# First units of a gated attention and routed experts kernel: one transfer for the second set of decay operands, narrower gate arithmetic, loads and gate rows in another order

## The chip, the cores and the metric

The kernel runs as one program on 1 core of one Trainium2 chip. The metric is the device time in microseconds (us); the median of the runs is compared. Engines are called PE (matmul; PEld is its weight load), DVE, ACT and POOL; SP only issues DMA transfers. POOL issues transfers too.

## The reference, cut to what matters

Two stages follow one another. The first is a gated linear attention over 4 batches, 8 heads, 768 steps and head size 40, with a stabiliser that runs along time:

```
for t in range(S):
    m_new = np.maximum(f_gate[:, :, t] + m, i_gate[:, :, t])
    f_stab = np.exp(f_gate[:, :, t] + m - m_new)
    i_stab = np.exp(i_gate[:, :, t] - m_new)
    C = f_stab * C + i_stab * np.einsum('bhd,bhe->bhde', vt, kt)
    n = f_stab * n + i_stab * kt
    h_tilde = np.einsum('bhde,bhe->bhd', C, qt)
    denom = np.maximum(np.abs(nq), 1.0)
    y[:, :, t] = o * h_tilde / denom
```

The second takes the 3072 rows of y (320 wide) to the best two of 8 experts each: noisy logits, a softmax over the two, `relu(x @ w1[e]) @ w2[e]` with a hidden width of 1024, weighted and added up.

## The kernel before, in words

**Units.** Time is cut into chunks of 64 steps. A unit is one chunk of two batches, so there are 24 units: 0 to 11 for the first pair of batches, 12 to 23 for the second. The loop over `i` runs unit `i` and prepares the next ones. What a unit needs: queries and keys `qk` (two transfers, 256 and 64 KB, line 170), values and keys `vk` (two of 162 KB, one from SP and one from POOL, line 175), the output gate `og` (160 KB, line 177). Each has four buffers; in the loop unit `i + 3` is loaded in iteration `i`. Buffers of `qk` are blanked once (`blank`, line 191), those of `vk` get zeros and unit matrices once (lines 263 to 268).

**Work of a unit, in PE's order.** `c_part` (line 381) makes the next state, `o_part` (390) the outputs, `e_part` (330) the decay exponents of unit `i + 2` in two halves, each followed by an Exp on ACT (333) that makes the weights `w`; `l_part` and `t_part` (433, 413) belong to the experts' logits; `s_part` (353, 350) makes the scores of unit `i + 2`. DVE makes `kd` (361, keys times the last decay of `w`), the three steps of the denominator (395 to 401) and the weighted scores `p` (367, or 371 for a pair's first unit). `o_part(i)` waits for `p` of its unit, `c_part(i)` for `kd`. ACT also makes the sigmoid of `og` in three steps (`sig_part`, 339), POOL the finished rows (402), which are sent off on line 405. Each engine takes its instructions in the order in which the program writes them.

**Gates.** `gate_math` (lines 212 to 234) turns f and i gates into decay sums: two scans and six other steps on DVE, eight in all, for a stretch of time, into `HL`. `gate_move` (line 236) takes 128 steps of `HL`, that is two units, to the operands `LE` and `RE` with three small transfers (16, 8 and 8 KB). `RE` and `LE` have two sets, used in turn, two units each. The constant part of a set, which never changes, is written once: `operands` (248, 250) on ACT, `heads` (257 on ACT, 259 on DVE). Before, the set of units 2 and 3 is filled by ACT and DVE as the first is. Gate stretches are 128 wide for the first two and 256 wide for the last two; the latter's steps are a generator, `gates2`, of which the loop takes some at places that `GATES` sets.

**Names in the rows.** `e(u)` below means the decay matmuls of unit `u`; the row `e<-re,le` of line 330 appears twice for each unit.

**Order and waits.** Nothing is reordered: the order of the program is that of each engine. Each queue issues in order, and an issue that waits holds back all behind it. Warm-up matmuls on zeros (line 712, `WARM`, `WARM2`, `WARM3`) fill PE at the start. After the units the experts follow, the first of which is begun in the last units' iterations.

Of the kernel before, what the change touches and what calls it, by code (L numbers as in the profile page):

```python
# [7 lines left out]
F32 = mybir.dt.float32  # L8
# [5 lines left out]
AF = mybir.ActivationFunctionType  # L14
OP = mybir.AluOpType
AX = mybir.AxisListType

B, H, S, D = 4, 8, 768, 40
NE, F, DM = 8, 1024, 320
L = 64  # L20
# [19 lines left out]
NR = NE - EF  # L40

STEP, SHARE = 0.19, 1.65
WARM, WARM2, WARM3 = 16, 5, 2
GATES = {0: 5, 2: 4, 3: 4}
LEAD = 2
TURN = 6
OR1 = (0, 6, 1, 2, 3, 4, 5)
# [5 lines left out]
GC = 2  # L53
# [12 lines left out]
def build(ctx, tc, qk, vk, og, fi, noise, wgn, w1, w2, cst, ce, out):  # L66
# [98 lines left out]
    def load_unit(u, what="kvg"):  # L165
        pr, c = divmod(u, NCH)
        if "k" in what:
            r = 0
            for a, step, n in DIMS:
                SP.dma_start(QK[u % 4][a:128:step], qk[pr, c, r:r + n])  # L170
                r += n
        if "v" in what:
            flat = VKS[u % 4].rearrange("p x c -> p (x c)")
            for p in range(2):
                (P if p else SP).dma_start(flat[64 * p:64 * p + 64, VW * p:VW * p + 648], vk[pr, c, p])
        if "g" in what:
            SP.dma_start(SG[u % 4], og[pr, c])
# [12 lines left out]
    def blank(i, q):  # L190
        q.memset(QK[i], 0.0)
# [8 lines left out]
    SP.dma_start(fit[:, :, 128:256], fi[:, :, 128:256])  # L200
    load_unit(0, "k")
    SP.dma_start(cs[:, 0:C_TRI], cst[:, 0:C_TRI])
    load_unit(0, "vg")
    P.dma_start(fit[:, :, 256:512], fi[:, :, 256:512])
    blank(2, P)

    def run(steps):
        for _ in steps:
# [29 lines left out]
    def gate_move(kk, q=(SP, SP)):  # L238
        pr, k = divmod(kk, GB)
        j = kk % 2  # L240
        src = HL[32 * pr:32 * pr + 32, :, k * GC * L:(k + 1) * GC * L].bitcast(F32)
        q[0].dma_start(LE[j][64:96, :, 64:128].bitcast(F32), src[:, 0].rearrange("r (c t) -> r c t", c=GC))
        for x in range(2):
            q[x].dma_start(RE[j][96 + x:97 + x].bitcast(F32), src[16 * x:16 * x + 16, 1])

    def operands(j, p, eng=None):
        if p is None:
            A.activation(LE[j][0:KE], cet[0:KE, None, E_L:E_L + 192].to_broadcast([KE, GC, 192]), AF.Copy)
        else:
            A.activation(RE[j][0:64, p].rearrange("r h (c t) -> r h c t", c=GC),  # L250
                         cet[0:64, None, None, 0:L].to_broadcast([64, H, GC, L]), AF.Copy)

    def heads(j, p, eng):
        o, i = RE[j][64:96, p], cet[64:96, E_H:E_H + H, None].to_broadcast([32, H, GC * L])
        x = cet[64:96, E_P + p:E_P + p + 1]
        if eng is A:
            A.activation(o, i, AF.Copy, scale=x)
        else:
            V.tensor_scalar(o, i, x, None, op0=OP.mult)


    def key_zeros(i):
        P.memset(VK[i][1][32:64, 0:328], 0.0)
# [2 lines left out]
    def keys(i):  # L266
        P.tensor_copy(VK[i][0][64:104, 328:648].rearrange("p (h d) -> p h d", h=H), ident[64:104, None, 64:104].to_broadcast([40, H, D]))
        P.tensor_copy(VK[i][1][0:64, 328:648].rearrange("p (h d) -> p h d", h=H), ident[0:64, None, 0:D].to_broadcast([64, H, D]))
# [5 lines left out]
    gate_move(0, (SP, P))  # L274
    operands(0, 0, A)
    operands(0, 1, A)
    heads(0, 0, A)
    heads(0, 1, A)
    load_unit(1)
    keys(0)  # L280
    keys(1)
    operands(1, None, A)
    operands(1, 0, A)
    run(gate_math(GC * L, 256))
    heads(1, 0, V)
    heads(1, 1, V)
    gate_move(1, (SP, P))
    load_unit(2, "k")
    blank(3, P)
    for i in range(2, 4):  # L290
        key_zeros(i)
        keys(i)
    load_unit(2, "vg")
    load_unit(3, "k")

    def constants():
        P.memset(W1L[0:64, 2].bitcast(F32), 0.0)
# [26 lines left out]
    def e_part(u, ps_=(0, 1), first=False):  # L324
        pr, c = divmod(u, NCH)
        j = (GB * pr + c // GC) % 2
        c = c % GC
        for p in ps_:
            ps = XTB if first and p else psum.tile([128, 512], F32, name="e")
            T.matmul(ps, LE[j][0:KE, c, 64 - 64 * p:192 - 64 * p], RE[j][0:KE, p, :, c * L:c * L + L], start=True, stop=True)  # L330
            if p == 0:
                W[u] = wk.tile([128, 2, H, L], F32, name="w", bufs=LEAD)
            A.activation(W[u][:, p].rearrange("p h t -> p (h t)"), ps, AF.Exp)  # L333

    def sig_part(u, ps_=(0, 1, 2)):

        g = SG[u % 4]
        for p in ps_:
            A.activation(g, g, (AF.Exp, AF.Ln, AF.Exp)[p], bias=float(p == 1), scale=(-1.0, 1.0, -1.0)[p])
# [4 lines left out]
    def s_part(u):  # L344
        q = QK[u % 4]
        for h in range(H):
            if whole(u) and h == 1:
                for p in range(2):
                    r = qrow[p]
                    T.matmul(SQ[u][:, p][r], cs[r, C_DIM:C_DIM + 64], q[r, 0], start=True, stop=True)  # L350
            for p in range(2):
                r = qrow[p]
                T.matmul(SQ[u][:, p][half[p], h, :], q[r, 1, h, :], q[r, 0, h, :], start=True, stop=True)  # L353
# [4 lines left out]
    def k_part(u):  # L358
        if u % NCH < NCH - 1:
            KD[u] = wk.tile([128, 2, H, D], F32, name="kd")  # L360
            V.tensor_mul(KD[u], VKS[u % 4][:, :, 328:648].rearrange("p x (h d) -> p x h d", h=H),
                         W[u][:, :, :, L - 1:L].to_broadcast([128, 2, H, D]))
# [346 lines left out]
    def warm(n):  # L709
        wp = psum.tile([128, 512], F32, name="o")  # L710
        for _ in range(n):
            T.matmul(wp, wz[:, 0:128], wz, start=True, stop=True)
# [3 lines left out]
    s_room(1)  # L716
    s_part(0)
    warm(WARM2)
    e_part(0, first=True)
    operands(1, 1, A)  # L720
    warm(WARM3)
    s_part(1)
    e_part(1, first=True)
    k_part(0)
    p_part(0)
    load_unit(3, "vg")
    SP.dma_start(fit[:, :, 512:], fi[:, :, 512:])
    SP.dma_start(wgt, wgn)
    gates2 = (s for t0 in (256, 512) for s in gate_math(t0, t0 + 256))

    def route(i):
        if 2 <= i <= NU + 1 and sum(GROUPS[GOF[i - 2]]) == i - 1:
# [93 lines left out]
    i = 0  # L826
    while i < NU - LEAD:
        unit[0] = i
        spent[0] = 0.0
        if 1 <= i and i + 3 < NU:  # L830
            load_unit(i + 3, "kv")
        if i:
            keep_rows(i - 1)
        if 1 <= i and i + 3 < NU:
            load_unit(i + 3, "g")
        if i % 2 == 0 and i and i // 2 + 2 < 2 * GB:
            gate_move(i // 2 + 2, (P, P) if i < XV else (SP, SP))

        if i in W1LD:
            piece_w1(W1LD.index(i))  # L840
        if i == W2AT:
            early_w2(0, 4)
        if i == 4:
            SP.dma_start(cs[:, C_TRI:], cst[:, C_TRI:])
        if i == 5:
            SP.dma_start(nzt, noise)
        while sent:
            SP.dma_start(*sent.pop())
        if not begun and done[0] >= E0U[0]:
            decode(0, E0S[1] // 128, 128 * E0U[0] > FIT)  # L850
            begun = 1
        if begun and late < len(tiles(0, 0)):
            gather(0, 0, tiles(0, 0)[late:late + 2])
            late += 2
            begun = 2
        if i == 6:
            constants()
            A.activation(spot, cs[:, C_N:C_N + 128], AF.Copy)
            A.activation(tri, cs[:, C_TRI:C_TRI + 128], AF.Copy)
            A.activation(ones, cs[:, C_ONE:C_ONE + 128], AF.Copy)  # L860
        asked = len(acts)
        k_part(i + 1)
        if i == 1:
            for _ in range(8 - GATES[0]):
                next(gates2)
            gate_move(2, (SP, P))
        fill(0.2, False)
        s_room(i + 2)
        c_part(i)
        if i:  # L870
            sig_part(i + 1, (0,))
        o_room(i)
        o_part(i)
        e_part(i + LEAD, (0,))
        act(asked)
        if i == 0:
            sig_part(0)
        f_part(i, lambda: fill(0.15, False))
        p_part(i + 1)
        t = l_part(i)  # L880
        w = r_part(t)
        b = None if w else b_part(t)
        if i:
            t_part(i - 1)
            tc_part(i - 1)
        lc_part(i, t, w)
        bc_part(t, b)
        if i < 2:
            s_part(i + 2)
            sig_part(i + 1, (1, 2) if i else (0, 1, 2))  # L890
            e_part(i + LEAD, (1,))
        else:
            e_part(i + LEAD, (1,))
            s_part(i + 2)
            act()
            sig_part(i + 1, (1, 2))
        route(i)
        fill((SHARE if i < NU - 3 else 0.6) - spent[0])
        if i in W1AT:
            next(pre1)  # L900
        for _ in range(GATES.get(i, 0)):
            next(gates2, None)
        if 6 <= i < 13:
            P.memset(XG[:, i - 6], 0.0)
        i += 1
# [471 lines left out]
```

## Time and profile before

| what | value |
|---|---|
| runs | 528.5, 529.3, 534.17 us; median 529.3 us |
| profiled execution | 529.1 us, span of the core 527.3 us |
| PE busy | 503.5 us (95% of the span) |
| DVE, ACT, POOL busy | 342.6, 247.5, 230.0 us |
| mean granted PE clock | 0.987 |

A busy share is an average over the whole span; the units lie in its first 125 us, the experts in the rest. The granted clock is a share of 2.4 GHz: 1.00 is that level, 0.50 is 1.2 GHz. Times in rows count from the start of the span. The table of stretches shows where PE stands still, the chain shows what it stood still for.

### The profile page before, as it was taken

What the parts mean: (1) busy time and instruction counts of PE and PEld (TensorE: products, weight loads), DVE (VectorE), ACT (ScalarE), POOL (GpSimd) and SP (SyncE); (2) the same over time, 40 slices, a digit from 0 to 9 for tenths busy, and PEclk for the clock granted to TensorE, in tenths of its full rate; (3) what the DMA queues carried; (4) which work ended last, traced back from release to release, by engine and by line L of the source; (5) the groups of instructions that cost most, each with busy time, mean ns of one, the idle gap of its engine ahead of it and who ended that gap; (6) DMA issues with size and microseconds to landing.
All of it is one profiled execution on the core that took longest, in us unless ns stands there. A gap on an engine that the chain in (4) does not pass through costs nothing.

```text
span 527.3 us, 13159 instructions
## 1 busy us (share of the span) xinstructions
PE 503.5 (95%) x5042; PEld 475.1 (90%) x5043; DVE 342.6 (65%) x949; ACT 247.5 (47%) x605; POOL 230.0 (44%) x298
## 2 busy tenths in 40 slices
PE   7789999999999899999999999999999999999994
PEld 3688888887988898999999999999999999999993
DVE  8876989999797377763765485377548447545410
ACT  7758878879613255432542354054325415515300
POOL 8638575364013736145415623460562255151043
PEclk9979999999999899999999999999999999999998
DMA  6879887776767527069229505931861583272033
GB/s 167 230 210 248 240 228 193 222 230 192 266 183 242 92 40 215 7 121 265 79 60 274 101 27 118 252 91 41 225 132 55 111 249 86 57 171 25 2 37 42
DMA packets 52341, 76.80 MB, mean 146 GB/s; under 512 B 10809, under 2 KB 42944, under 8 KB 52272
## 3 DMA queue, kind: packets, MB, share of 16 engines
q1 hardware_dynamic: 40048, 53.04, 33.8%
q0 software_dynamic: 12224, 22.84, 21.7%
q8 instruction: 42, 0.69, 0.6%
q14 instruction: 27, 0.22, 0.1%
HBM read 52.27 MB, written 17.48 MB: 132 GB/s over the span
## 4 chain that ended last, share of the span: by engine, by line
PE 79%; DVE 11%; ACT 3%; DMA 3%; issue 1%; another core or an unknown queue 1%; SPq 1%; POOL 0%; POOLq 0%; DVEq 0%
PE s L1013 24%; PE e L1013 11%; PE o L1042 5%; PE o L1043 5%; PE o L1044 5%; PE st L1043 5%; PE st L1042 5%; PE st L1044 5%; PE o L390 3%; PE s L353 2%; DVE p L367 2%; PE e L330 2%; PE st L381 2%; PE xt L433 1%; PE xt L413 1%
## 5 line engine op out<-in xcount | busy, mean ns | idle before, releaser
L1065 POOL DMA_INDIRECT y_out<-y,tok x53 | 87.1, 1643 | 192.6 <-DVE y L1055 191.5
L1022 ACT ACTIVATE hh<-s 128x384 fp32r<-128x384 f32 (+3 forms) x91 | 42.8, 470 | 89.8 <-PE s L1013 83.4
L1013 PE MATMUL s<-xh,w1h 128*128 128x384 f32 (+5 forms) x273 | 76.8, 338 | 0.7 <-DVE vc L467 0.7
L785 POOL DMA_INDIRECT xg<-rows,tok x53 | 59.1, 1116 | 28.2 <-issue 14.3
L1025 DVE SCALAR_TENSOR_TENSOR hlo<-s,hh 128x384 fp32r<-128x384 f32 (+3 forms) x91 | 47.8, 525 | 27.2 <-ACT hh L1022 23.5
L1013 PE MATMUL s<-xh,w1l 128*128 128x384 f32 (+5 forms) x273 | 62.5, 336 | 0.7 <-DVE xh L819 0.7
L1043 PE MATMUL o<-w2l,hh 128*128 128x320 f32 x184 | 57.3, 312 | 0.0
L1042 PE MATMUL o<-w2h,hh 128*128 128x320 f32 x184 | 57.2, 311 | 0.0
L1044 PE MATMUL o<-w2h,hlo 128*128 128x320 f32 x184 | 56.6, 308 | 0.0
L1043 PE MATMUL st<-w2l,hh 128*128 128x320 f32 x176 | 55.2, 314 | 0.7 <-issue 0.7
L1044 PE MATMUL st<-w2h,hlo 128*128 128x320 f32 x176 | 54.5, 310 | 0.8 <-issue 0.7
L1042 PE MATMUL st<-w2h,hh 128*128 128x320 f32 x176 | 54.7, 311 | 0.0
L1013 PEld LDWEIGHTS s<-xh,w1h 128*128 128x128 f32 x273 | 48.9, 188 | 2.6 <-PE s L1013 0.9
L1013 PEld LDWEIGHTS s<-xh,w1l 128*128 128x128 f32 x273 | 47.9, 188 | 2.2 <-DVE xh L819 0.9
L1013 PE MATMUL s<-xl,w1h 128*128 128x384 f32 (+5 forms) x182 | 46.4, 336 | 0.0
L1022 ACT ACTIVATE hh<-e 128x384 fp32r<-128x384 f32 (+3 forms) x45 | 21.3, 473 | 42.5 <-PE e L1013 38.5
L1055 DVE TENSOR_SCALAR y<-st,gw 128x320 f32<-128x320 f32 x22 | 12.1, 551 | 43.8 <-PE st L1044 43.8
L1055 DVE TENSOR_SCALAR y<-o,gw 128x320 f32<-128x320 f32 x23 | 12.6, 550 | 42.1 <-PE o L1044 42.1
L1013 PE MATMUL e<-xh,w1h 128*128 128x384 f32 (+5 forms) x135 | 38.8, 342 | 0.0
L402 POOL TENSOR_TENSOR xr<-tm,vk 128x320 f32<-128x320 f32 x24 | 20.9, 869 | 38.2 <-ACT w L333 11.2
L390 PE MATMUL o<-vk,p 128*64 128x41 f32 (+2 forms) x768 | 28.5, 231 | 6.9 <-DVE p L367 4.1
L1042 PEld LDWEIGHTS o<-w2h,hh 128*128 128x128 f32 x184 | 34.6, 188 | 0.3 <-DVE y L1055 0.2
(237 smaller groups left out, 1262.8 us busy)
## 6 DMA issues: line engine op xcount, KB each, us to landing
raw<-w_in SPq DMA_DIRECT2D x7, 1280.0 KB
raw<-w_in SPq DMA_DIRECT2D x7, 1024.0 KB
qk<-qk_in SPq DMA_DIRECT2D x24, 256.0 KB
raw<-w_in SPq DMA_DIRECT2D x19, 256.0 KB
y_out<-zrow SPq DMA_DIRECT2D x15, 320.0 KB
vk<-vk_in POOLq DMA_DIRECT2D x24, 162.0 KB
vk<-vk_in SPq DMA_DIRECT2D x24, 162.0 KB
vk<-og_in SPq DMA_DIRECT2D x24, 160.0 KB
```

Source lines behind the costliest of these rows:

```text
L330: T.matmul(ps, LE[j][0:KE, c, 64 - 64 * p:192 - 64 * p], RE[j][0:KE, p, :, c * L:c * L + L], start=True, stop=True)
L390: T.matmul(OQ[u][half[p], h, :], PP[u][n, p, h, :], VK[u % 4][p][n, h * 41:h * 41 + 41], start=True, stop=True)
L402: P.tensor_mul(XR[u], tm.rearrange("p h d -> p (h d)"), SG[u % 4])
L785: P.indirect_dma_start(out=XG[0:rows_of(t), t], out_offset=None, in_=XD[0:n], in_offset=bass.IndirectOffsetOnAxis(ap=token(e, t), axis=0), ...
L1013: T.matmul(ps[:, 0:n], l, r, start=i == 0, stop=i == len(ops) - 1)
L1022: A.activation(hi, x, AF.Relu)
L1025: V.scalar_tensor_tensor(lo, x, 0.0, hi.bitcast(F32), op0=OP.max, op1=OP.subtract)
L1042: T.matmul(ps, HH[:, j, c], W2H[:, j], start=j == 0, stop=False)
L1043: T.matmul(ps, HH[:, j, c], W2L[:, j], start=False, stop=False)
L1044: T.matmul(ps, HLO[:, j, c], W2H[:, j], start=False, stop=j == 7)
L1055: V.tensor_scalar(y[0:n], ps[0:n], GW[e][0:n, t:t + 1], None, op0=OP.mult)
L1065: st = P.indirect_dma_start(out=out, out_offset=bass.IndirectOffsetOnAxis(ap=token(e, t), axis=0), in_=y[0:n], in_offset=None, compute_op= ...
```

## The change

It does six things.

1. The constant part of the second `RE` set (96 partitions by 2048 floats, 768 KB) is copied from the first set by one transfer of SP. Four instructions go: two of ACT (250) and two of DVE (259).
2. Gate arithmetic of the last 512 steps is in four stretches of 128 instead of two of 256, 32 DVE instructions instead of 16. Six steps are written ahead of the loop; then 4, 4, 4, 4, 5 and 5 steps at the end of iterations 0 to 5, behind that iteration's `p`.
3. SP asks for `qk` of unit 1 ahead of the first gate rows, and for `og` of the first units later; `vk` and `og` of units 2 and 3 are also in another order. POOL blanks the fourth `qk` buffer ahead of its zeros.
4. Scores of unit 1 come ahead of the decay matmuls of units 0 and 1; there are fewer warm-up matmuls (3, 2 and 2 instead of 5 and 2).
5. The sigmoid of unit 0 is written ahead of the Exps of unit 1, that of unit 1 behind the second Exp of unit 2.
6. `gate_move` for units `i + 3` and `i + 4` is issued in odd iterations instead of even ones: each one a unit later than before, from the third on. The move for units 4 and 5 is at the head of iteration 1, all three transfers on POOL, where it was inside iteration 1 with two on SP and one on POOL.

```diff
-WARM, WARM2, WARM3 = 16, 5, 2
-GATES = {0: 5, 2: 4, 3: 4}
+WARM, WARM2, WARM3 = 16, 3, 2
+GATES = (6, 4, 4, 4, 4, 5, 5)
...
     SP.dma_start(cs[:, 0:C_TRI], cst[:, 0:C_TRI])
-    load_unit(0, "vg")
+    load_unit(0, "v")
     P.dma_start(fit[:, :, 256:512], fi[:, :, 256:512])
     blank(2, P)
+    blank(3, P)
+    load_unit(1, "k")
...
-    heads(0, 0, A)
-    heads(0, 1, A)
-    load_unit(1)
+    heads(0, 0)
+    heads(0, 1)
+    load_unit(1, "v")
     keys(0)
     keys(1)
+    load_unit(0, "g")
+    load_unit(2, "k")
+    SP.dma_start(RE[1][0:96].bitcast(F32), RE[0][0:96].bitcast(F32))
     operands(1, None, A)
-    operands(1, 0, A)
     run(gate_math(GC * L, 256))
-    heads(1, 0, V)
-    heads(1, 1, V)
     gate_move(1, (SP, P))
-    load_unit(2, "k")
-    blank(3, P)
+    load_unit(2, "v")
+    load_unit(1, "g")
     for i in range(2, 4):
         key_zeros(i)
         keys(i)
-    load_unit(2, "vg")
     load_unit(3, "k")
+    load_unit(2, "g")
+    load_unit(3, "vg")
+    gates2 = (s for t0 in range(256, S, 128) for s in gate_math(t0, t0 + 128))
+
+    def gates_on(n):
+        for _ in range(n):
+            next(gates2, None)
+
+    gates_on(GATES[0])
...
     warm(WARM2)
+    s_part(1)
     e_part(0, first=True)
-    operands(1, 1, A)
     warm(WARM3)
-    s_part(1)
+    sig_part(0)
     e_part(1, first=True)
+    warm(WARM3)
     k_part(0)
     p_part(0)
-    load_unit(3, "vg")
...
-    gates2 = (s for t0 in (256, 512) for s in gate_math(t0, t0 + 256))
...
-        if i % 2 == 0 and i and i // 2 + 2 < 2 * GB:
+        if i % 2 and i // 2 + 2 < 2 * GB:
             gate_move(i // 2 + 2, (P, P) if i < XV else (SP, SP))
...
-        if i == 1:
-            for _ in range(8 - GATES[0]):
-                next(gates2)
-            gate_move(2, (SP, P))
...
-        if i == 0:
-            sig_part(0)
...
             s_part(i + 2)
+            e_part(i + LEAD, (1,))
             sig_part(i + 1, (1, 2) if i else (0, 1, 2))
-            e_part(i + LEAD, (1,))
...
-        for _ in range(GATES.get(i, 0)):
-            next(gates2, None)
+        if i < 6:
+            gates_on(GATES[i + 1])
```

Three places show what moves. The first is SP's queue near its start, from the `vk` of unit 0 on; before:

```order
L175 DMA vk_109<-vk_in 64x648
L177 DMA vk_109<-og_in 128x320
L242 DMA le_99<-hl 32x2x64
L244 DMA re_97<-hl 1x16x128
L170 DMA qk_106<-qk_in 64x1024
L170 DMA qk_106<-qk_in 16x1024
L175 DMA vk_110<-vk_in 64x648
L177 DMA vk_110<-og_in 128x320
L242 DMA le_100<-hl 32x2x64
L244 DMA re_98<-hl 1x16x128
L170 DMA qk_107<-qk_in 64x1024
L170 DMA qk_107<-qk_in 16x1024
```

and now (numbers 105, 106, 107 are the `qk` of units 0, 1, 2; 109 to 112 the `vk` of units 0 to 3; 97 and 98 the two `RE` sets):

```order
L175 DMA vk_109<-vk_in 64x648
L170 DMA qk_106<-qk_in 64x1024
L170 DMA qk_106<-qk_in 16x1024
L244 DMA le_99<-hl 32x2x64
L246 DMA re_97<-hl 1x16x128
L175 DMA vk_110<-vk_in 64x648
L177 DMA vk_109<-og_in 128x320
L170 DMA qk_107<-qk_in 64x1024
L170 DMA qk_107<-qk_in 16x1024
L281 DMA re_98<-re_97 96x2048
L244 DMA le_100<-hl 32x2x64
L246 DMA re_98<-hl 1x16x128
```

The queries of unit 1 stand three issues earlier, and the copy between the two sets stands behind the queries of unit 2.

The second is DVE around the weighted scores of unit 1, whose row is the one with 128x1024; before:

```order
L401 SCALAR_TENSOR_TENSOR tm<-dn,o 128x320
L367 TENSOR_TENSOR p<-s,w 128x1024
L214 SCALAR_TENSOR_TENSOR xg<-raw_120,xg 64x256
L217 TENSOR_TENSOR xg<-raw_120,xg 64x256
L219 TENSOR_TENSOR xg<-xg 64x256
L224 SCALAR_TENSOR_TENSOR xg<-raw_120,xg 64x256
L226 TENSOR_TENSOR xg<-raw_120,xg 64x256
L361 TENSOR_TENSOR kd<-vk_111,w 128x640
L228 TENSOR_TENSOR xg<-xg 64x256
L231 CAST hl<-xg 64x2x256
L233 SCALAR_TENSOR_TENSOR hl<-hl,raw_120,xg 64x2x256
```

and now:

```order
L406 SCALAR_TENSOR_TENSOR tm<-dn,o 128x320
L372 TENSOR_TENSOR p<-s,w 128x1024
L233 CAST hl<-xg 64x2x128
L235 SCALAR_TENSOR_TENSOR hl<-hl,raw_120,xg 64x2x128
L216 SCALAR_TENSOR_TENSOR xg<-raw_120,xg 64x128
L219 TENSOR_TENSOR raw_120<-raw_120,xg 64x128
L366 TENSOR_TENSOR kd<-vk_111,w 128x640
L400 RECIPROCAL dn<-o 128x8
L402 SCALAR_TENSOR_TENSOR dn<-dn 128x8
L406 SCALAR_TENSOR_TENSOR tm<-dn,o 128x320
L372 TENSOR_TENSOR p<-s,w 128x1024
```

Between the weighted scores of units 1 and 2 stand four narrow gate steps where eight wide ones stood, and the gates for units 4 and 5 are done with the second of the four.

The third is POOL from the rows of unit 0 (`xr` of `vk_109`) on; before:

```order
L402 TENSOR_TENSOR xr<-tm,vk_109 128x320
L175 DMA vk_109<-vk_in 64x648
L405 DMA rows<-xr 128x320
L244 DMA re_97<-hl 1x16x128
L402 TENSOR_TENSOR xr<-tm,vk_110 128x320
L175 DMA vk_110<-vk_in 64x648
L405 DMA rows<-xr 128x320
L242 DMA le_100<-hl 32x2x64
L244 DMA re_98<-hl 1x16x128 x2
```

and now:

```order
L407 TENSOR_TENSOR xr<-tm,vk_109 128x320
L175 DMA vk_109<-vk_in 64x648
L410 DMA rows<-xr 128x320
L244 DMA le_99<-hl 32x2x64
L246 DMA re_97<-hl 1x16x128 x2
L407 TENSOR_TENSOR xr<-tm,vk_110 128x320
L175 DMA vk_110<-vk_in 64x648
L410 DMA rows<-xr 128x320
L407 TENSOR_TENSOR xr<-tm,vk_111 128x320
```

All three transfers of the move for units 4 and 5 are POOL's now, behind the rows of unit 0, and the move for units 6 and 7 no longer stands behind the rows of unit 1 but behind those of unit 2.

## Rows read from the trace of the kernel before

**Rows 1.** The page's first part: busy time, share of the span and instructions of PE; and from the table of stretches one of 100 us (columns: stretch, its length, busy us and instructions of PE, PEld, DVE, ACT, POOL, granted clock, DMA share, GB/s).

```profile
PE 503.5 (95%) x5042; PEld 475.1 (90%) x5043; DVE 342.6 (65%) x949; ACT 247.5 (47%) x605; POOL 230.0 (44%) x298
...
200.00:300.00 100.00, 100.00 (x600) 95.75 (x599) 60.64 (x149) 39.14 (x99) 45.57 (x52) 1.00 0.56 143
```

**Rows 2.** The same table for short stretches of the first 45 us.

```profile
20.00:22.50 2.50, 2.50 (x63) 1.94 (x64) 2.43 (x6) 2.44 (x7) 0.00 (x0) 1.00 1.09 244
22.50:25.00 2.50, 0.41 (x22) 0.32 (x16) 2.43 (x6) 1.85 (x5) 1.67 (x3) 1.00 0.89 249
25.00:27.50 2.50, 1.90 (x33) 1.70 (x34) 1.53 (x5) 0.00 (x0) 2.30 (x5) 0.64 0.76 226
27.50:30.00 2.50, 2.50 (x15) 2.04 (x17) 2.43 (x4) 1.03 (x3) 1.94 (x3) 0.50 0.99 290
30.00:32.50 2.50, 2.50 (x55) 2.37 (x57) 1.48 (x3) 1.45 (x5) 0.00 (x0) 0.50 0.96 254
...
40.00:45.00 5.00, 5.00 (x118) 4.57 (x117) 3.81 (x8) 4.05 (x10) 3.24 (x7) 1.00 0.91 248
```

**Rows 3.** The chain that ended last, in order of time (start us, us, what), from the first 60 us.

```profile
0.74 2.32 DMA raw<-fi_in
...
8.41 3.21 DMA qk<-qk_in
...
22.11 0.74 DVE hl L233
...
23.18 0.38 SPq L242
23.61 3.21 DMA re<-hl
26.96 0.76 PE e L330
...
33.67 0.74 issue
```

**Rows 4.** Timeline of PE, the first decay matmul of units 2, 3, 5 and 6 (start us, us, engine, line, operation, tile, shape, count; in brackets the idle time before, and its releaser).

```profile
15.29 0.49 PE L330 MATMUL e<-re,le 98*128 98x512 f32 x1
...
19.80 0.51 PE L330 MATMUL e<-re,le 98*128 98x512 f32 x1
...
34.77 0.51 PE L330 MATMUL e<-re,le 98*128 98x512 f32 x1
...
39.18 0.51 PE L330 MATMUL e<-re,le 98*128 98x512 f32 x1
```

**Rows 5.** Timeline of the start, all engines (same columns): issues of the `qk` of units 1 and 2, the last step of the second narrow gate stretch, the part of the constant operands that DVE writes, the sigmoids of units 0 and 1, the first scores of unit 2.

```profile
7.83 1.17 SPq L170 DMA_DIRECT2D qk<-qk_in  x2
...
8.93 0.60 DVE L233 SCALAR_TENSOR_TENSOR hl<-hl,raw,xg 64x256 fp32r<-64x256 f32 x1
...
9.57 2.44 DVE L259 TENSOR_SCALAR re<-raw 32x1024 fp32r<-32x1024 f32 x2
...
11.79 1.17 SPq L170 DMA_DIRECT2D qk<-qk_in  x2
...
16.31 2.83 ACT L339 ACTIVATE vk<-vk 128x320 f32<-128x320 f32 x6
...
16.61 0.27 PE L353 MATMUL s<-qk 64*64 64x64 f32 x2 [0.82 <-DMA qk<-qk_in]
```

**Rows 6.** Timeline, DVE: the first step of a narrow and of a wide gate stretch, the work of units 1 and 2 (same columns).

```profile
6.21 0.47 DVE L214 TENSOR_TENSOR_SCAN xg<-raw,xg 64x128 f32<-64x128 f32 x1
...
15.85 0.49 DVE L401 SCALAR_TENSOR_TENSOR tm<-dn,o 128x320 f32<-128x320 f32 x1
...
17.38 0.73 DVE L214 TENSOR_TENSOR_SCAN xg<-raw,xg 64x256 f32<-64x256 f32 x1
...
20.48 0.81 DVE L361 TENSOR_TENSOR kd<-vk,w 128x640 f32<-128x640 f32 x1
...
23.61 1.22 DVE L367 TENSOR_TENSOR p<-s,w 128x1024 f32<-128x1024 f32 x1
```

**Rows 7.** Timeline, POOL: issues of one gate move in iteration 6 (`le` once, `re` twice), and the rows sent in iterations 5, 7, 9 and 11.

```profile
42.59 0.57 POOL L405 DMA_DIRECT2D rows<-xr  x1
...
46.81 0.55 POOL L242 DMA_DIRECT2D le<-hl  x1
47.37 0.99 POOL L244 DMA_DIRECT2D re<-hl  x2
...
52.46 0.57 POOL L405 DMA_DIRECT2D rows<-xr  x1
...
61.48 0.57 POOL L405 DMA_DIRECT2D rows<-xr  x1
...
71.63 0.56 POOL L405 DMA_DIRECT2D rows<-xr  x1
```

**Rows 8.** Timeline, PE: the first decay matmuls of units 8, 10, 12 and 14.

```profile
48.05 0.50 PE L330 MATMUL e<-re,le 98*128 98x512 f32 x1
...
57.36 0.51 PE L330 MATMUL e<-re,le 98*128 98x512 f32 x1
...
67.11 0.49 PE L330 MATMUL e<-re,le 98*128 98x512 f32 x1
...
76.44 0.50 PE L330 MATMUL e<-re,le 98*128 98x512 f32 x1
```

More of the change, by code (lines that the diff above doesn't have):

```diff
@@ L251, in operands, with heads @@
                          cet[0:64, None, None, 0:L].to_broadcast([64, H, GC, L]), AF.Copy)
[L253 to L259, printed above, removed]
+    def heads(j, p):
+        A.activation(RE[j][64:96, p], cet[64:96, E_H:E_H + H, None].to_broadcast([32, H, GC * L]), AF.Copy,
+                     scale=cet[64:96, E_P + p:E_P + p + 1])
     def key_zeros(i):
```

## The prediction

> **What bounds the kernel now.** I read the page's first part, then the table of stretches, the chain of waits, and last the timeline of the stretch that the first two point to. PE is busy for 95% of the span, and in the experts it never stands still [rows 1]. So a time saved or lost in the first units is handed on to the end, and the question is what the first 45 us hold. In the table PE is busy for all of 20 to 22.5 us, for 0.41 of the next 2.5 us, and after that its granted clock is 0.64 and then 0.50, where it had been 1.00 [rows 2]. The chain says what PE stood still for: the last step of the first wide gate stretch ends at 22.85, SP issues the gate rows up to 23.61, they take 3.21 us, and the decay matmul of unit 4 starts at 26.96 [rows 3].
>
> What that costs is read from the first decay matmul of each unit. Units 5 and 6 are 39.18 - 34.77 = 4.41 us apart, which I take for an undisturbed unit. Units 3 and 4 are 26.96 - 19.80 = 7.16 us apart, units 4 and 5 34.77 - 26.96 = 7.81 us [rows 3, 4]. The two hold 2.75 and 3.40 us too much: the wait, and then the half clock with a hole of 0.74 us in which PE waited for nothing that the profile shows [rows 3]. 6.15 us is all that a change of the first units can win here, unless it starts them sooner.
>
> **The change part by part.**
>
> *Queries of unit 1 and the sigmoids.* SP asks for these queries at 7.83 [rows 5]; three issues of some 0.6 us fewer stand ahead, so they come about 2 us sooner. Nothing is won: the first decay matmuls wait for gate rows whose time stays. The sigmoid of unit 0, half of a pair's 2.83 us [rows 5], now stands ahead of the Exps of unit 1 and takes up what ACT saves. I count 0. Fewer warm-ups: 0, as they fill waits; if the clock fell there it would be the second rival.
>
> *The copy of the operand set.* It takes 2.44 us from DVE [rows 5] and two instructions from ACT. On DVE six narrow steps take the place: a narrow stretch goes from 6.21 to 9.53, 3.32 us for eight [rows 5, 6], so six take 2.5 us, and I count 0. The copy itself is new. Four issues (values and gate of one unit, queries of unit 2) stand between the first gate rows, behind which SP was free at 7.83, and the copy: it is issued at about 7.83 + 4 x 0.6 = 10.2. Its 786 kB take 2.7 us at 290 GB/s and 3.2 at 244, two rates of stretches with the DMA engines busy [rows 2]. The trace has no transfer of this kind. From below: it lands as a pair of query transfers does, 3.21 us after its issue [rows 3], at 13.4, and costs nothing. From above: 1.15 MB asked for just before it go first, which at 244 GB/s takes 4.7 us from about 7.5 on, and the copy runs at half the rate beside POOL's transfers: 12.2 + 6.4 = 18.6. I take 12.2 + 3.2 and 1 us for the end of the transfer, 16.4. The decay matmul of unit 2 was at 15.29 [rows 4], so this is 1.1 late.
>
> *Gates for units 4 and 5.* DVE ended `tm` of unit 0 at 16.34 [rows 6]; I take 16.7. The weighted scores of unit 1 take 1.22 [rows 6], up to 17.9, two narrow steps 0.84, and these gates are done at 18.8, not at 22.85. Two more steps, `kd` at 0.81, the denominator at 0.9, and the weighted scores of unit 2 end at 22.6, not at 24.83 [rows 6]. The late copy is hidden behind DVE here.
>
> *Their move.* It now waits on POOL behind the rows of unit 0 and two issues, which end at about 18.7, so nothing is queued longer. The three issues take 0.55 + 0.99 [rows 7]; the last starts at 19.9. A landing took 3.21 us for the same rows [rows 3], and 4.2 for the second query transfer of unit 2, issued at about 12.4 and waited for until 16.61 [rows 5]. So the rows are there at 23.1 to 24.1. PE reaches them behind the outputs of unit 2, at 22.6 + 1.1 = 23.7. I take 24.3 for the decay matmul of unit 4, a little over the later landing, as the copy's data use the same engines: **2.66 us won**. The bounds are 23.7 and, if the rows wait for all of the copy, 23.1 + 3.2 = 26.3.
>
> *The clock.* Without the two us of standing still the clock stays at 1.00, and of the 3.40 us between units 4 and 5 the hole of 0.74 stays, as no part of the change touches it: **2.66 us won**.
>
> *Narrow steps.* Four narrow stretches take 4 x 3.32 = 13.3 us of DVE; two wide ones take 2 x 4.66 = 9.3 (17.38 to 22.85 without the 0.81 of `kd`) [rows 3, 6]. In iterations 0 to 5, 26 steps of 0.42 make 1.8 us a unit, and with 2.9 of the unit's own DVE work 4.7, against 4.41 on PE. Up to 0.3 us for each of four units is not covered: between 0 and 1.2, near the upper end as DVE has no other slack, **1.0 us lost**.
>
> *Gate moves one unit later.* POOL sends the rows of iteration 5, 7, 9 and 11 at 42.59, 52.46, 61.48 and 71.63 [rows 7]; behind them the moves will stand whose first users are the decay matmuls at 48.05, 57.36, 67.11 and 76.44 [rows 8]. That leaves 5.46, 4.90, 5.63 and 4.81 us. Needed are 0.57 + 0.55 + 0.49 for the issues and 3.21 to 4.2 to land: 4.82 to 5.81. So these moves, which had a unit to spare, are late by 0 or by 0.35, 0.91, 0.18 and 1.00, up to 2.4 us; for the four that SP issues later I take the same bound. Between 0 and 4.9 us I take **1.0 us lost**, near the lower end, since 3.21 is the row for this very transfer.
>
> The sum: 529.1 - 2.66 - 2.66 + 1.0 + 1.0 = **525.8 us**. It is made against the profiled execution, whose span is 527.3; its 529.1 stands 0.2 under the median of 529.3. By the bounds of the terms it lies between 529.1 - 3.26 - 2.66 = 523.2 and 529.1 - 0.66 - 2.66 + 1.2 + 4.9 = 531.9.
>
> **The rivals.**
>
> *All of it is on time.* The copy lands before PE gets there, unit 4 starts at 23.1, the hole goes with the half clock, DVE's extra steps fit and no move is late: 529.1 - 3.9 - 3.40 + 0.5 = 522.3. For it: from 40 to 45 us, under the same loads, PE is never still [rows 2]. Against it: DVE at 4.7 us a unit. 2 in 10.
>
> *A wait takes the place of the old one.* The DMA engines were busy for 0.76 to 1.09 of these stretches [rows 2]. If all queues share one line, the copy puts 3.2 us on everything behind it, and the gate rows of unit 4 land at 26.3 to 27.3, where they landed before; PE stands still from 24 on and its clock falls as it did. Or the copy lands at 18.6 and the clock falls there. Then nothing is won, DVE's extra steps hide in the wait, and the late moves cost their 1.0: 529.1 + 1.0 = 530.1. 2 in 10. The Trainium skill (Trainium Kernel Development and Optimization, Key Constraints) speaks for this: transfers from SP, ACT and POOL run on the same 16 engines, and another queue saves issue time alone. It speaks against the change, and by it the time is 530.1. The skill's page DMA: Bandwidth & Descriptors (Queues, rings and completion order) has each engine take turns between queues, so POOL's small rows need not wait for all of the copy; by that it is 525.8. No row here tells the two apart.
>
> *Slower: every gate move late.* If landings in the loaded units take 4.2 us or more, each of eight moves stops PE for 0.6 us at its even unit. That decides from 5 us between rows and use on, which two of the four distances are under. With the second rival's start it is 529.1 + 4.9 = 534.0, with my own start 529.1 - 5.32 + 1.0 + 4.9 = 529.7. Against it: landings of 3.21. 1 in 10.
>
> **How the numbers follow.** My forecast has 5 in 10, the rivals 2, 2 and 1. The predicted time is the forecast's, 525.8. The range 522.0 to 531.0 takes in most of the first rival and all of the second and leaves out the slow end of the third. About 1%, here 5.3 us, is what a measurement of this kernel can tell from no change: faster means under 524.0, slower over 534.6. Faster: most of the first rival and the lower edge of the forecast, 0.26. Slower: half of the third, 0.05. The rest is the same, 0.69.
>
> **What would show it.** In the profile after: `HL` of units 4 and 5 done before 20 us; the copy landed by 17; decay matmul of unit 4 near 24.3 and a granted clock of 1.00 throughout 15 to 40; units 2 to 6 spaced at 4.4 to 4.8 us with PE waiting for DVE; short waits of `e` for `re` at even units from 8 on. It is wrong if `e` of unit 2 waits past 17.5, if a stretch of half clock is left before 45 us, if waits for gate rows sum to over 2 us, or if the experts do not hand the gain on.

## The result, and the profile after

The change makes the kernel slower. Its median is 536.96 us (531.48 to 540.6, 18 runs), that of the kernel before on the same chip 529.81 us (526.64 to 534.17, 18 runs); the ratio is **1.0121, 95% interval 1.0096 to 1.0146**. The forecast was 525.8 us with a range of 522.0 to 531.0; slower than 534.6 us had a chance of 0.05. The ratios, here and below, leave out single runs more than 1.5% above the fastest of their kernel, here three of the changed kernel's 18, while the medians take in all runs.

The profiled execution of the changed kernel took 532.53 us with a span of 530.7, against 529.1 and 527.3 before. It is one of the shortest of its runs. The mean granted clock goes with the time: 0.992 in the run of 531.48 us, 0.972 in the run of 540.6. So the trace shows one of the milder executions: a loss of 3.4 us, where the ratio makes it some 6.4 (1.21% of 529.8). The 18 executions have a mean clock of 0.978, those of the kernel before in the experiments about 0.987. The difference of 0.009 over 530 us is some 5 us, an estimate by which more than half of the loss comes as a lower clock. Some traces of the experiments show that part.

The busy time of PE on the page is what it was [rows 1]:

```profile
PE 503.3 (95%) x5042; PEld 473.8 (89%) x5043; DVE 343.1 (65%) x963; ACT 245.5 (46%) x603; POOL 229.3 (43%) x297
```

The first decay matmul of the units in the timeline of PE, which answers to [rows 4, 8] (units 2, 3, 4, 5, 6, 8, 10, 12, 14 and 23):

```profile
18.71 0.47 PE L335 MATMUL e<-re,le 98*128 98x512 f32 x1 [2.68 <-DMA re<-hl]
...
23.75 0.51 PE L335 MATMUL e<-re,le 98*128 98x512 f32 x1
...
27.70 0.49 PE L335 MATMUL e<-re,le 98*128 98x512 f32 x1
...
32.62 0.50 PE L335 MATMUL e<-re,le 98*128 98x512 f32 x1
...
38.09 0.47 PE L335 MATMUL e<-re,le 98*128 98x512 f32 x1 [0.98 <-DMA re<-hl]
...
46.85 0.50 PE L335 MATMUL e<-re,le 98*128 98x512 f32 x1
...
56.86 0.47 PE L335 MATMUL e<-re,le 98*128 98x512 f32 x1 [0.31 <-DMA re<-hl]
...
67.78 0.47 PE L335 MATMUL e<-re,le 98*128 98x512 f32 x1 [1.14 <-DMA re<-hl]
...
78.29 0.47 PE L335 MATMUL e<-re,le 98*128 98x512 f32 x1 [1.16 <-DMA re<-hl]
...
125.33 0.50 PE L335 MATMUL e<-re,le 98*128 98x512 f32 x1
```

Read as differences to before, this is the history of the loss. Unit 2 is 3.42 us late and unit 4 still 0.74. Unit 5 is 2.15 us early, unit 6 1.09, unit 8 1.20: part of the gain that was hoped for is there, 1.20 at unit 8 of the 5.32 us that the sum counted as won. Then it is lost: unit 10 is 0.50 early, unit 12 0.67 late, unit 14 1.85 late. The last unit, 23, started at 121.95 before, so it is 3.38 late, which the experts hand on to the end (3.4 us). Between units 8 and 23 the changed kernel loses 4.6 us. Unit 23 in the kernel before:

```profile
121.95 0.50 PE L330 MATMUL e<-re,le 98*128 98x512 f32 x1
```

The stretches of the start show how the gain was made and paid for [rows 2]; columns as there:

```profile
15.00:17.50 2.50, 1.02 (x30) 0.91 (x30) 2.19 (x5) 0.85 (x2) 0.71 (x4) 1.00 1.02 243
17.50:20.00 2.50, 1.29 (x33) 1.08 (x35) 1.98 (x5) 0.60 (x1) 2.45 (x5) 0.96 1.01 261
20.00:22.50 2.50, 2.50 (x51) 1.95 (x45) 0.54 (x1) 1.20 (x3) 0.68 (x2) 0.50 1.03 271
22.50:25.00 2.50, 2.50 (x54) 2.21 (x56) 1.31 (x5) 2.42 (x7) 0.02 (x1) 0.85 1.10 261
25.00:27.50 2.50, 2.50 (x91) 2.19 (x81) 2.43 (x6) 1.71 (x4) 1.93 (x3) 1.00 0.83 216
```

PE now stands still from 15 to 20 us (busy for 2.31 of 5), and the half clock comes at 20, not at 26. The chain of waits names the cause, and then one step of the same kind at even units [rows 3]:

```profile
10.57 0.56 SPq L281
...
11.97 6.49 DMA re<-hl
...
18.71 0.47 PE e L335
...
32.03 5.93 DMA re<-hl
...
53.14 3.63 DMA re<-hl
...
62.52 5.13 DMA re<-hl
...
73.83 4.33 DMA re<-hl
...
94.08 5.21 DMA re<-hl
```

L281 issues the copy. The last gate row of unit 2 is issued behind it on SP and lands 6.49 us later, at 18.46. The other rows are gate moves that the change puts one iteration later (of units 6, 10, 12, 14 and 18), each on the chain because PE waits for it.

Timeline of DVE and POOL at the places of [rows 6, 7] (the gates of units 4 and 5 done, `kd` and weighted scores of unit 2; the row store of iteration 7 and the move behind it):

```profile
18.35 0.48 DVE L235 SCALAR_TENSOR_TENSOR hl<-hl,raw,xg 64x256 fp32r<-64x256 f32 x1
...
21.96 0.83 DVE L366 TENSOR_TENSOR kd<-vk,w 128x640 f32<-128x640 f32 x1 [2.41 <-ACT w L338]
...
24.75 1.22 DVE L372 TENSOR_TENSOR p<-s,w 128x1024 f32<-128x1024 f32 x1
...
51.54 0.57 POOL L410 DMA_DIRECT2D rows<-xr  x1
52.11 0.55 POOL L244 DMA_DIRECT2D le<-hl  x1
52.65 0.98 POOL L246 DMA_DIRECT2D re<-hl  x2
```

### The profile page after: what moved, and what is told of

Same layout as the page of the kernel before. It is cut to its first block, busy times and chain, and to the rows that moved or that the text cites. A ratio compares the mean times of both kernels' runs of the same rounds, so it can differ in the third digit from the quotient of the medians.

```text
span 530.7 us, 13166 instructions
## 1 busy us (share of the span) xinstructions
PE 503.3 (95%) x5042; PEld 473.8 (89%) x5043; DVE 343.1 (65%) x963; ACT 245.5 (46%) x603; POOL 229.3 (43%) x297
## 4 chain that ended last, share of the span: by engine, by line
PE 72%; DVE 9%; DMA 8%; ACT 3%; POOL 3%; issue 2%; SPq 1%; POOLq 0%; DVEq 0%
PE s L1011 23%; PE e L1011 11%; DMA re<-hl 6%; PE o L1040 5%; PE o L1041 5%; PE o L1042 5%; PE st L1041 5%; PE st L1042 5%; PE st L1040 5%; DVE p L372 2%; DMA le<-hl 1%; PE o L395 1%; DVE ob L649 1%; PE e L335 1%; DMA vk<-vk_in 1%
## 5 line engine op out<-in xcount | busy, mean ns | idle before, releaser
L338 ACT ACTIVATE w<-e 128x512 f32<-128x512 f32 x46 | 27.6, 600 | 20.8 <-PE e L335 20.3
```

## The experiments

Each ratio is to the kernel before on the same chip. My theory from this trace (A): the gate moves, now asked for one iteration later, cost most of it; the copy costs a little. Theory B: the copy costs most of it. "Unit 4" below means its first decay matmul.

**e1, the late moves alone**, in the kernel before:

```
-        if i % 2 == 0 and i and i // 2 + 2 < 2 * GB:
+        if i % 2 and i > 1 and i // 2 + 2 < 2 * GB:
```

> The kernel before, with only this changed: gate moves for units 6 on are issued one iteration later. Theory A (the late moves make the loss): slower than before by 4 to 8 us, with PE waiting for the gate rows at the even units from 8 on, each by 0.5 to 2 us. Theory B (the copy makes the loss): within 1 us of before.

Measured: 531.35 against 524.34 us, 1.0147 [1.010, 1.0194], some 7.7 us by the ratio and 5 to 10 by its interval. This one line costs about as much as the whole change. Its trace has a mean granted clock of 0.96 from 60 to 100 us, where before had 1.00.

**e2, the change with its moves at even iterations as before** (the gate steps dealt out to suit):

```
-GATES = (6, 4, 4, 4, 4, 5, 5)
+GATES = (6, 5, 5, 4, 4, 4, 4)
-        if i % 2 and i // 2 + 2 < 2 * GB:
+        if (i == 1 or i and i % 2 == 0) and i // 2 + 2 < 2 * GB:
```

> The changed kernel with the gate moves back in even iterations, and the gate steps taken a little sooner (5, 5, 4, 4, 4, 4 a unit) so that they are done in time. Theory A: faster than the changed kernel by 4 to 8 us and 0 to 2 us under the kernel before, as the decay matmul of unit 5 came 2.15 us sooner than before. Theory B: still 3 to 6 us over the kernel before.

Measured: 523.89 us, 0.9998 [0.9968, 1.0028]. The loss is gone, and no gain is left either.

**e3, the change without the copy**, and **e4, without the copy and with the moves of e2**. ScalarE makes the second set:

```
-    SP.dma_start(RE[1][0:96].bitcast(F32), RE[0][0:96].bitcast(F32))
     operands(1, None, A)
+    operands(1, 0, A)
+    heads(1, 0)
...
+    operands(1, 1, A)
     e_part(1, first=True)
+    heads(1, 1)
```

and the sigmoid of unit 0 stands in the loop again (e4 has the edit of e2 besides).

> The changed kernel without the copy: ACT makes all of the second operand set itself (four instructions, 4.4 us), and the sigmoid of unit 0 is behind the first Exp of unit 2 as before. Theory A: the first decay matmul of unit 2 comes near 15.5 us instead of 18.7, but the late moves remain; 1 to 3 us under the changed kernel and 2 to 5 us over the kernel before. Theory B: at or under the kernel before.

> Both of these: no copy, and gate moves in even iterations. Theory A: fastest of the four, 2 to 5 us under the kernel before, granted clock 1.00 from 10 to 100 us. Theory B: the same as without the copy alone. If neither is all of it (the narrow gate steps cost more on DVE than they win), it stays at the kernel before.

Measured: e3 528.68 us, 1.0085 [1.0048, 1.0123]; e4 522.84 us, 0.9966 [0.993, 1.0002]. Both pairs, the change against e3 and e2 against e4, put the copy (with the sigmoid's place) at 0.3 to 0.4%, which the intervals do not tell from nothing. Unit 4 is no earlier in e4 than the 26.96 of before [rows 3]:

```profile
26.93 0.47 PE L336 MATMUL e<-re,le 98*128 98x512 f32 x1 [1.00 <-DMA re<-hl]
```

Here the traces also show the part of the loss that the change's own trace lacks. The stretch of 60 to 100 us, first of e3 and then of e4:

```profile
60.00:100.00 40.00, 37.49 (x857) 33.65 (x854) 33.10 (x120) 30.00 (x80) 20.30 (x37) 0.93 0.73 201
```

```profile
60.00:100.00 40.00, 37.49 (x896) 33.50 (x899) 36.31 (x124) 32.06 (x88) 20.24 (x35) 1.00 0.80 220
```

PE is busy equally long, but gets through 857 matmuls instead of 896, with a granted clock of 0.93. In e3 the decay matmuls wait 1.60 us for gate rows up to 56.84 and 1.52 us up to 78.21; the granted clock is 0.62 and 0.52 in the two stretches of 2 us from 58 on, 0.74 and 0.50 in the two from 78 on, and 1.00 from 62 to 78. Not every wait has this behind it: after one of 1.14 us up to 59.56 in e1 the clock stays at 1.00. A late move costs its wait, and in some executions half clock behind it as well.

**e6, e1 with the late moves at the head of their iteration**, ahead of its loads and the row store:

```
+        if i % 2 and i > 1 and i // 2 + 2 < 2 * GB:
+            gate_move(i // 2 + 2, (P, P) if i < XV else (SP, SP))
         if 1 <= i and i + 3 < NU:
             load_unit(i + 3, "kv")
...
-        if i % 2 and i > 1 and i // 2 + 2 < 2 * GB:
-            gate_move(i // 2 + 2, (P, P) if i < XV else (SP, SP))
```

> e1 (late gate moves alone) with the late moves issued at the head of the odd iteration, ahead of that iteration's key load, query load and row store, so that POOL and SP reach them some 1 to 1.5 us sooner. Theory A (the distance decides): the loss of e1 (1.0147) falls to 1.004 to 1.010, in proportion to the waits that go. Rival (it is the transfers that are slow while the unit's own loads run, and asking a microsecond sooner only makes them slower): 1.012 to 1.016.

Measured: 528.18 against 528.53 us, 0.9992 [0.9971, 1.0012]. More than A expected: all of the loss is gone. POOL's timeline for the move of unit 10, in e1 and then in e6:

```profile
52.90 0.53 POOL L175 DMA_DIRECT2D vk<-vk_in  x1
53.42 0.57 POOL L405 DMA_DIRECT2D rows<-xr  x1
53.99 0.55 POOL L242 DMA_DIRECT2D le<-hl  x1
54.53 0.98 POOL L244 DMA_DIRECT2D re<-hl  x2
```

```profile
52.08 0.57 POOL L242 DMA_DIRECT2D le<-hl  x1
52.64 0.98 POOL L244 DMA_DIRECT2D re<-hl  x2
53.60 0.54 POOL L175 DMA_DIRECT2D vk<-vk_in  x1
54.13 0.57 POOL L405 DMA_DIRECT2D rows<-xr  x1
```

The decay matmul of unit 10 starts at 59.56 in e1, after a wait of 1.14 us for these rows, and at 57.56 in e6, with none. Without the wait, e1 has 4.43 us from the first of these issues to that matmul and e6 5.48; 1.10 is what the two issues take that no longer stand ahead. The last transfer also landed sooner, 2.31 us after its issue instead of 4.41, by the trace's record of its end; for unit 6 that is 5.58 instead of 5.72. How much either of the two is worth, the earlier issue or the shorter landing, e6 does not tell. What the decay matmuls waited for between 20 and 130 us (us, times), in the change, in e1 and in e6:

```profile
DMA re<-hl: 6.0, 6
```

```profile
DMA re<-hl: 4.5, 4
```

```profile
DMA re<-hl: 1.5, 1
```

The 1.5 us left in e6 is the old wait of unit 4, which e1 (1.56 of its 4.5) and the kernel before (0.6) have too.

**e8, e1 with the late moves on SP**:

```
-            gate_move(i // 2 + 2, (P, P) if i < XV else (SP, SP))
+            gate_move(i // 2 + 2)
```

> e1 (late gate moves alone) with all late moves issued by SP instead of POOL for units 6 to 14. Theory A (the distance decides): 1.008 to 1.018, as in e1, since SP's transfers took 2 to 6 us as well. Rival (POOL's place in line, behind its own key load, row store and xr, is what is late): 1.000 to 1.005.

Measured: 533.25 us (7 runs), 1.0071 [1.0037, 1.0104]. It lies between the two and settles little: the other queue helps by less than a better place in POOL's own. SP has its own loads ahead of the move, and the decay matmuls still wait 2.7 us in 3 units for gate rows, 0.43 of it at unit 4.

**e12, the changed kernel whole with its moves at the head**, as in e6 (in the change all of them, unit 4's in iteration 1 too, stand behind that iteration's loads and row store):

```
+        if i % 2 and i // 2 + 2 < 2 * GB:
+            gate_move(i // 2 + 2, (P, P) if i < XV else (SP, SP))
         if 1 <= i and i + 3 < NU:
             load_unit(i + 3, "kv")
...
-        if i % 2 and i // 2 + 2 < 2 * GB:
-            gate_move(i // 2 + 2, (P, P) if i < XV else (SP, SP))
```

> The changed kernel whole, with one thing moved: the gate moves stand at the head of their odd iterations, ahead of that iteration's key load, query load and row store, as in e6. Theory A (the gate moves' place makes the change's loss, the copy costs 0.2 to 0.4% and the start's gain about pays it): as e2, 0.998 to 1.003, against 1.0121 for the change; waits of the first decay products of units 6 to 22 for their gate rows fall from some 6 us in sum to under 2. Rival (in the changed kernel the denser unit leaves less room than before's, and a move asked for a microsecond sooner is still late): 1.006 to 1.010.

Measured: 529.41 against 528.93 us, 1.0008 [0.9986, 1.003]. In its trace no decay matmul between 20 and 130 us is charged with a wait for gate rows at all; it is the shortest of its twelve executions. Two lines moved up by a few take the change from 1.2% slower to no difference.

**e10, the copy alone** in the kernel before, in place of the four operations that make the constant part of the second set:

```
+    SP.dma_start(RE[1][0:96].bitcast(F32), RE[0][0:96].bitcast(F32))
     operands(1, None, A)
-    operands(1, 0, A)
     run(gate_math(GC * L, 256))
-    heads(1, 0, V)
-    heads(1, 1, V)
...
-    operands(1, 1, A)
```

> The kernel before with the copy alone: the second set of decay operands by one transfer of 786 kB issued ahead of unit 2's gate rows, in place of ScalarE's and VectorE's five operations; nothing else changed. The prediction's term: the copy lands at 16.4 us and the first decay product of unit 2 starts 1.1 us late, at 16.4, with the loss hidden behind VectorE later: 0.999 to 1.001. From the pairs of runs with and without it (after against e3, e2 against e4): the rows of unit 2 land behind the copy at 17.5 to 18.5, that product starts at 17.7 to 18.7, and the total rises by 0.2 to 0.4%: 1.002 to 1.005. Rival (VectorE, free of 2.44 us of operand work, runs its first steps earlier and pays it back): 0.997 to 1.000.

Measured: 531.26 against 528.83 us, 1.0028 [1.0001, 1.0056], so the cost is only just clear of nothing. Its first decay matmul of unit 2, in the longest of its executions (535.18 us):

```profile
18.66 0.76 PE L328 MATMUL e<-re,le 98*128 98x512 f32 x1 [3.25 <-DMA re<-hl]
```

That is what the pairs said, at the place they said. The prediction's 16.4 for this matmul is out by 2.3 us.

**e7, e4 with the gate steps 256 wide**:

```
-GATES = (6, 5, 5, 4, 4, 4, 4)
+GATES = (4, 4, 2, 3, 3, 0, 0)
-    gates2 = (s for t0 in range(256, S, 128) for s in gate_math(t0, t0 + 128))
+    gates2 = (s for t0 in range(256, S, 256) for s in gate_math(t0, t0 + 256))
```

> e4 with the gate arithmetic of units 4 to 11 in steps 256 wide (16 steps) in place of 128 wide (32 steps). The prediction took 1.0 us (0 to 1.2) for the added instructions of the narrow steps: by it this runs 0.5 to 1.2 us faster than e4, 0.994 to 0.9965. Rival (VectorE's added work lies in gaps): within 0.3 us of e4. Other rival (a wide step holds VectorE longer ahead of kd and p): 0.5 to 1.5 us slower than e4, 0.998 to 1.000.

Measured: 529.02 against 528.53 us, 1.001 [0.9984, 1.0036], where e4 had 0.9966. No gain from wide steps, so the 1.0 us that the prediction put on narrow ones does not appear. The comparison is not clean: in e7 unit 4 waits 1.45 us for its rows (e4: 1.00) and the clock falls to 0.68 and 0.63 between 27.5 and 32.5 us.

**e5, e4 with unit 4's rows first**: the last two of their eight gate steps run ahead of the loop, and their move at the head of unit 0's iteration:

```
-GATES = (6, 5, 5, 4, 4, 4, 4)
+GATES = (8, 3, 5, 4, 4, 4, 4)
-        if (i == 1 or i and i % 2 == 0) and i // 2 + 2 < 2 * GB:
+        if i % 2 == 0 and i // 2 + 2 < 2 * GB:
```

> e4 with the last two gate steps of units 4 and 5 run ahead of the loop (where VectorE stands idle for 2.3 us before its first kd) and the move of unit 4's gate rows issued at the head of unit 0's iteration, on POOL, which does nothing there from 16 to 20 us. Theory A (the distance between the issue of a gate move and its use is what costs): the first decay matmul of unit 4 loses the wait that e4 still has there (1.00 us, released by the transfer of the gate rows) and starts at 25.5 to 26.1 us instead of 26.93; total 0.3 to 1.3 us under e4, 0.994 to 0.997 of the kernel before. Rival (the wait only gives way to another, VectorE's p or ScalarE's w of unit 3): within 0.3 us of e4.

Measured: 525.24 against 528.53 us, **0.995 [0.9933, 0.9967]**, the largest gain of all; only e9, a variant of it, also has its whole interval under 1. Units 4 and 5 in its trace:

```profile
25.29 0.49 PE L336 MATMUL e<-re,le 98*128 98x512 f32 x1
...
30.22 0.50 PE L336 MATMUL e<-re,le 98*128 98x512 f32 x1
```

No wait, 4.93 us apart, and a granted clock of 1.00 from 10 to 100 us. A's 25.5 to 26.1 for unit 4 was even a little late. The twelve executions have a mean clock of 0.994, the 30 of before 0.988; 0.006 of 528 us is some 3 us, an estimate that covers the whole gain.

**e9, e5 with the first decay matmul ahead of the scores of unit 1**, as before:

```
-    s_part(1)
     e_part(0, first=True)
-    warm(WARM3)
     operands(1, 1, A)
+    warm(WARM3)
+    s_part(1)
```

> e5 with the first decay product of unit 0 back ahead of the scores of unit 1 in TensorE's order, as the kernel before has it. In e5 the two scores of unit 1 wait for their queries and the decay product stands behind them: first decay products of units 0 and 2 at 11.79 and 16.74 us, in the kernel before 10.28 and 15.29. The prediction put this reordering at nothing. If it was not nothing, the products of units 2 and 4 start 0.5 to 1.4 us sooner than in e5 and the total is 0.4 to 1.4 us under e5, 0.9925 to 0.9945 of the kernel before. Rival (what follows is bound by the rows of unit 4 and by VectorE anyway): within 0.3 us of e5.

Measured: 526.91 against 528.83 us, 0.9968 [0.9942, 0.9994]: no better than e5. In its trace units 2 and 4 start 0.4 and 0.2 us sooner, but PE waits 1.59 us for POOL's `xr` at 37.05, behind the issues of unit 8's move, and runs at half clock after that. Whether that recurs in its other runs I cannot say.

**e11, the kernel before with unit 4's rows first**, without copy, late moves or new order:

```
-GATES = {0: 5, 2: 4, 3: 4}
+GATES = (6, 3, 5, 4, 4, 4, 4)
-    heads(1, 0, V)
-    heads(1, 1, V)
+    heads(1, 0, A)
...
+    gates2 = (s for t0 in range(256, S, 128) for s in gate_math(t0, t0 + 128))
...
+    gates_on(GATES[0])
...
     e_part(1, first=True)
+    heads(1, 1, A)
     k_part(0)
     p_part(0)
+    gates_on(2)
...
-        if i % 2 == 0 and i and i // 2 + 2 < 2 * GB:
+        if i % 2 == 0 and i // 2 + 2 < 2 * GB:
...
```

> The kernel before with one part of the change alone, and ahead of its place there: gate steps of units 4 and 5 128 wide and run ahead of the loop (6) and behind the first p (2), unit 4's gate rows asked for at the head of unit 0's iteration on POOL; to make room on VectorE the two head operations of the second set go to ScalarE. No copy, no late moves, queries and TensorE's order as before. Expected: first decay product of unit 4 at 24.0 to 25.0 us instead of 26.96 and units 4 to 5 apart by 4.4 to 5.0 instead of 7.82, with no half clock in 20 to 45 us: 4 to 6 us, 0.989 to 0.993. Rival (the seconds of ScalarE and VectorE that are moved ahead make the units 0 to 3 late by as much): 0.995 to 1.000, as e4 and e5.

Measured: 528.33 against 528.83 us, 0.9999 [0.9968, 1.003]: no gain, and a number in the rival's range. Units 2 and 3 do start later than before, by 0.45 and 0.68 us (15.74 and 20.48), but unit 4 starts at 25.05 us, close to what was expected, and unit 5 only at 32.82. Timeline of PE, the stretch behind it, and the instruction queue's line in the DMA view of 28 to 30 us:

```profile
28.44 0.86 PE L396 MATMUL o<-vk,p 104*64 104x41 f32 x23
32.23 0.66 PE L396 MATMUL o<-vk,p 104*64 104x41 f32 x8 [2.92 <-issue]
32.82 0.80 PE L336 MATMUL e<-re,le 98*128 98x512 f32 x1
```

```profile
30.00:32.00 2.00, 0.00 (x0) 0.00 (x0) 0.20 (x1) 0.00 (x0) 0.00 (x0) 1.00 1.03 239
32.00:34.00 2.00, 1.77 (x13) 1.60 (x12) 0.94 (x4) 0.35 (x1) 0.00 (x0) 0.50 0.63 217
```

```profile
q8 instruction: 1, 0.02, 3.7%
```

PE stops in the middle of a group of matmuls, waits for nothing that the profile records, and goes on at half clock. The hole, and the clock behind it, eat what the earlier rows won in this execution; whether the other eleven have them is not known.

## Why the prediction was wrong

*The gate moves one unit later: taken 1.0, bound 4.9, measured some 7.7 us by e1, 6.5 by the change against e2 (1.0121 - 0.9998) and 6.0 against e12 (1.0121 - 1.0008).* This is the step that failed. The room was read rightly: 4.90 us from the row store to the use at unit 10, less the issues of 0.57, 0.55 and 0.49 us, leaves 3.29 from the last issue on; it was 3.72 with the wait (53.14 to 56.86). The landing was not: 3.21 came from the start of the kernel, and in the units the same transfer took 5.93, 3.63, 5.13, 4.33 and 5.21 us, so that the decay matmuls waited 6.0 us for it in six units. The DMA engines were no idler at that start, 0.77 busy against 0.70 to 0.94 in these five, so their busy share alone does not say how long a landing takes.

No row of before showed more: these moves had a unit to spare, nobody waited for them, so they stood on no chain. I took the one landing that had a row for typical of nine that had none. Yet the trace of before records when each transfer ends, though no view prints it for these: the last one of the moves for units 6 to 16 landed 4.07, 4.55, 6.48, 3.94, 5.04 and 4.47 us after its issue, all over 3.21 and four over the 4.2 of the bound. The term could have been sized from there. Two things were put at nothing besides: the move of unit 6, late by 0.98 us, and the half clock that a wait can bring (e1, e3). The third rival had the mechanism and even its point, 5 us from rows to use, and got 1 in 10; its price of 4.9 was under what came too.

*The copy: taken 1.1 us late and hidden behind DVE.* It was 3.42 late at unit 2, and it was not hidden: ACT's `w` came late and DVE's `kd` of unit 2 waited 2.41 us for it, so the weighted scores of unit 2 ended at 25.97, not at 22.6 (before 24.83). The error was to ask when the copy lands; the trace records its end at 17.51, not 16.4. What PE waited for were the rows of unit 2, issued behind it on the same queue, and they were done at 18.46, close to the copy's upper bound of 18.6. In the total the copy costs 0.3% (e10, interval 0.0 to 0.6%). The second rival thus came true at unit 2 rather than at unit 4. The two pages of the Trainium skill that were weighed there are not told apart by this: the taking of turns between queues (DMA: Bandwidth & Descriptors, Queues, rings and completion order) could not help rows on the copy's own queue. One transfer of this move went by POOL's queue, but it was issued at 9.91, ahead of the copy, and no run puts such rows on another queue behind it.

*Gates of units 4 and 5, done at 18.8:* right, 18.83. *Their move, last issue at 19.9:* 20.2. *Unit 4 at 24.3, 2.66 won:* wrong, 27.70. The weighted scores ahead of it were late by the copy; and its rows took 5.31 us from the last issue (by the trace's record they landed at 25.49), where 3.21 to 4.2 had been counted. Without the copy nothing is won here either (e4: 26.93, with a wait of 1.00 us for these rows). It is won in e5, which has all eight gate steps ahead of the loop and asks for the rows in unit 0's iteration: there unit 4 starts at 25.29, 1.67 sooner than before.

*Clock, 2.66 won between units 4 and 5:* right in place, 4.92 apart instead of 7.81, with the hole gone too. But the half clock had only moved, to 20 to 25 us.

*Narrow steps, 1.0 lost:* not borne out by e7. *Order of TensorE's work, 0:* by e9 nothing in the total. *Queries and sigmoids, 0:* not shown, as no run changes them alone.

*The experts hand the difference on:* right, 3.38 us at unit 23 and 3.4 at the end.

Three of the four signs that were to show it wrong stood in the trace: the decay matmul of unit 2 past 17.5, half clock before 45 us, and waits for gate rows of 6.0 us against the limit of 2.

## What to carry to other kernels

A transfer for which nobody waits has no row in the chain, so before its slack is spent its landing time must be found in its own stretch, not borrowed from the one transfer that has a row. If it must be asked for later, put its issue at the head of the queue's work for that iteration: here that alone was worth 1.1% (1.0121 against 1.0008). And ask of a large transfer not only when it lands but which small ones are queued behind it.

## What was not expected of the hardware

The same small gate rows took 3.21 us to land at the start of the kernel before and up to 5.93 between the loads of later units of the changed one.

In e11 PE stood still for 2.92 us inside a group of 31 matmuls, with no recorded wait, and the chain of e10 has a step of the same length:

```profile
34.84 2.92 issue
```

In both, one packet of the instruction queue (`q8`) runs as the hole begins, in a stretch of 2 us in which the DMA engines are 0.94 (e10) and 1.08 (e11) busy. That PE was waiting for its next instructions behind the data is a reading of these rows; no run tests it. Against it: 19 such packets run between 20 and 130 us in the kernel before, and its hole of 0.74 us [rows 3] has none beside it (33 to 36 us).
